# Denominators spread by DMA, a projection bank lent to score units, FFN rows moved, and a shifted pass shared with GpSimd

## The chip, the cores and the metric

The kernel runs on one core of one Trainium2 chip. The metric is the device time of one execution in microseconds (us); lower is better. Times are medians of several executions, and a profile is one execution of its own.

## The reference

`x` is 2048 tokens of 640 values (bf16). The output is `x` plus an attention part plus a feed-forward part (FFN), both on the same normalised `xn`.

```python
def _A_ref(x, wq, wk, wv, wo):
    B, S, D = x.shape
    H = 32
    Dh = D // H
    q = (lambda x, *d: x.transpose(*d))((x @ wq).reshape(B, S, H, Dh), 0, 2, 1, 3)
    k = x @ wk
    v = x @ wv
    scores = jnp.einsum("bhqd,bkd->bhqk", q, k) * (Dh ** -0.5)
    p = _softmax(scores, axis=-1)
    o = jnp.einsum("bhqk,bkd->bhqd", p, v)
    return (lambda x, *d: x.transpose(*d))(o, 0, 2, 1, 3).reshape(B, S, H * Dh) @ wo
...
    h = jnp.einsum("bsd,df->bsf", x, w1) + b1
    r = jnp.where(h > zero, h, zero)
    h = r * r
    out = jnp.einsum("bsf,fd->bsd", h, w2) + b2
...
xn = _layernorm(x, axis=-1)
return x + _A_ref(xn, A_wq, A_wk, A_wv, A_wo) + _B_ref(xn, B_w1, B_b1, B_w2, B_b2)
```

There are 32 query heads of 20 values and a single key and value head; F is 1536. The heart of the work is 32 x 2048 x 2048 exponentials.

## The kernel before

The queries are cut into 4 chunks of 512 tokens (`qc`) and the heads into 8 groups of 4 (`g`); a chunk and a group make one of 32 **blocks**. A block has 16 **tiles**, one for each 128 keys, and a tile has 4 **units**, one for each head: a score matrix of 128 keys by 512 queries, which fills one bank of PSUM. There are 2048 units (L728).

Two engines turn scores into probabilities. *A tiles* go to ScalarE: `S_QK` (L738) makes two or three units in neighbouring banks, and one ACTIVATE (`S_EXP`, L790) takes the exponential of all of them into `PT`. *D tiles* go to VectorE. `S_D` (L820) puts one unit at a time in a bank of its own, `S_P1` (L875) converts it to an integer in `T8`, whose bits read as bf16 are a rough power of two, and `S_PH` (L901) makes four shifted copies of the whole tile of 2048 columns in `PB`. The PV product weighs the four with `PH_W`, so that their errors cancel. `QUOTA` says how many tiles of each block are D tiles, 115 of 512.

PSUM has 8 banks. 0 to 2 and 3 to 5 are two rotating sets for `S_QK`; the third bank of each (`XD` = 2, `DB` = 5) serves either an exponential of three banks or a D unit. `PVB` = 6 gathers the PV products of a block (`S_PV`, L967) and `MB` = 7 serves the **projection rows**, taken by `S_MISC` (L1049) from a list in order of due position: queries (QT, 31 after the first), the FFN's first product (FFN, 48), output rows (OUT, 24) and the last chunk's first halves (P1, 8). Each ends in an evacuation by VectorE.

At the end of a block `norm` (L984) divides the PV sum by its denominator, a row of the same sum: VectorE transposes PSUM to `Tn` (L987) and takes reciprocals (L991), GpSimd multiplies in two pieces (L993), and VectorE transposes back to `OTn` (L1013). GpSimd also squares the FFN's hidden rows, two pieces each (L617). Output rows add the residual from `x_sb`, which stays in SBUF.

The order of all instructions on all engines is worked out as the program is written, by a planner (`Sched`, L99) with fixed durations; each engine then runs its list in order and waits on semaphores. GpSimd's pieces are marked `under`: the planner starts each together with a long VectorE instruction that is not marked `port` (`beneath`, L223). Shifted passes are marked `port` and are not planned beside a GpSimd piece.

Of the kernel before, what the change touches and what calls it, by code (L numbers as in the profile page):

```python
# [6 lines left out]
F32 = mybir.dt.float32  # L7
# [33 lines left out]
QUOTA = [1, 3] + [4, 3, 4] * 9 + [4, 4, 4]  # L41
RING = 20
NT8 = 3
NPB = 5
NQS = 4
EVP = 1
DLEAD = 0.45
DWAIT = 120.0
DALONE = 1500.0
DBEHIND = (1.5, 0.0)  # L50
QLATE = 0.15
PG, PAT = 4, 28.4

SEM_NS = 60.0
PE_WIN = 3420.0
PE_MISC = 9000.0
# [28 lines left out]
class Req:  # L85


    def __init__(self, alts, deps, prio, name="", mode=None, deadline=None, rows=None, after=0.0, cols=0.0, even=False, port=False, under=False):
        self.alts = alts if isinstance(alts, list) else [alts]
        self.deps, self.prio, self.name, self.mode = deps, prio, name, mode  # L90
        self.deadline, self.rows, self.after = deadline, rows, after
        self.cols, self.even, self.port, self.under = cols, even, port, under
# [7 lines left out]
class Sched:  # L100
# [17 lines left out]

    def room(self, t, c):
        tot = self.load(t) + c  # L120
        for s_, c_ in self.win:
            if tot <= PE_MISC:
                break
            if s_ > t - PE_WIN:
                tot -= c_
                t2 = s_ + PE_WIN
                t = max(t, t2)
        return t
# [19 lines left out]
    def run(self):  # L148
        while self.streams:
# [7 lines left out]
            cands = []  # L157
            for st in self.streams:
                r = st[1]
                if isinstance(r, Until):  # L160
                    continue
                rr = r() if callable(r) else r
                if rr is None:
                    continue
                deps = rr.deps() if callable(rr.deps) else rr.deps
                if deps is None or rr.under:
                    continue
                t0 = max([d.done + SEM_NS for d in deps] + [rr.after])
                best = None
                for k, (eng, dur, lat, ins) in enumerate(rr.alts):  # L170
                    est = max(self.free[eng], t0)
                    if eng == "pool" or rr.port:
                        est = max(est, self.port)
                    if rr.even:
                        est = self.room(est, rr.cols)
                    if eng == "pe":
                        dur = self.pe_cost(rr, dur)
                    if best is None or est + dur < best[0]:
                        best = (est + dur, est, dur, k, eng)
                cands.append((best[1], best[2], rr, deps, best[3], best[4], st))  # L180
            if not cands:
                raise RuntimeError("stuck at %.0f: %s" % (self.now, [s[2] for s in self.streams]))
# [70 lines left out]
    def resolve(self, newsem):  # L253
# [37 lines left out]
        for e in self.ENG:  # L291
            n = 0
            for op in self.lists[e]:
                if op.dma is not None:
                    op.sig, op.sem, op.amt, op.val = True, newsem("d_" + op.dma), 16, 16
                elif op.sig:
                    n += 1
                    op.sem, op.amt, op.val = sems[e], 1, n

    def emit(self, eng, e):  # L300
        for op in self.lists[eng]:
# [7 lines left out]
            for f in op.ins:  # L309
                ins = f(e)  # L310
            if op.sig and op.ins:
                ins.then_inc(op.sem, op.amt)
# [5 lines left out]
def bass_parallel_sum__grouped_kv_mqa__dense_activation_squared_relu__prompt_kernel(nc, A_x, A_wq, A_wk, A_wv, A_wo, B_x, B_w1, B_b1, B_w2, B_b2, out):  # L318
    es = ExitStack()
    with es:  # L320
# [3 lines left out]
        x_sb = sb("x_sb", [128, ST, D], BF16)  # L324
# [21 lines left out]
        PB = sb("PB", [128, NPB, HPG, 512], I16)  # L346
        Tn = sb("Tn", [128, 2, 512], F32)
        rd = sb("rd", [128, 2, 16], F32)
        T2 = sb("T2", [128, 2, 512], BF16)
# [37 lines left out]
        def dma(eng, name, fn, deps, land):  # L387
            def gen():
                op = yield Req((eng, 60.0 if eng == "sp" else 500.0, land, [fn]), deps, 0, name)
                op.dma = name  # L390
                done[name] = op
            sc.spawn(gen(), name)
# [131 lines left out]
        def groups(gl, n, b_, deps, p, name, m=32, gdeps=None):  # L524
            v = None
            for k, (L, R) in enumerate(gl):
# [3 lines left out]
                elif gdeps is not None:  # L530
                    dd = dd + gdeps[k]
                v = yield Req(("pe", PE512 if n > 400 else PE320, (PE512 if n > 400 else PE320) + PELAT, col4(L, R, n, b_, k == 0, k == len(gl) - 1, m)),
                              dd, p, name, mode="col", cols=512.0 if n > 400 else 320.0, even=p >= 3)
# [89 lines left out]
        olast = {}  # L623

# [14 lines left out]
        def out_tail(v, st, hh, in1, b_, extra=()):  # L639
# [5 lines left out]
            olast[(st, hh)] = w  # L645
            if (st, 1 - hh) in olast:
# [8 lines left out]
        def u_OUT(qc, st, hh, b_):  # L655
# [7 lines left out]
            yield from out_tail(v, st, hh, x_sb[:, st, cs], b_)  # L663

        def u_P1(st, hh, gs, b_):
# [5 lines left out]
            v = yield Req(("dve", 450.0, 491.0, [lambda e: e.tensor_tensor(out=part[:, st % 4, cs], in0=ps[:, b_, 0:320], in1=x_sb[:, st, cs], op=ALU.add)]), [v], EVP, f"PE1_{st}_{hh}")  # L671
            done[f"PP{st}_{hh}"] = v
            bank[b_].last = [v]
# [7 lines left out]
        def u_FULL(st, hh, b_):  # L681
# [4 lines left out]
            yield from out_tail(v, st, hh, x_sb[:, st, cs], b_)  # L686
# [51 lines left out]
        def S_QK():  # L738
            k = 0
            slot = 0  # L740
            while apos[0] < len(aunits):
# [4 lines left out]
                n = 2 if busy[b3] or ("DBfree" if b3 == DB else "XDfree") not in done or d_behind() > DBEHIND[k % 2] else 3  # L746
# [64 lines left out]
        mbusy = [0]  # L811
        gates = [b + m / float(QUOTA[b]) - DLEAD for b, m, t in dtiles] + [float(NBLK)]

        def d_behind():
            p = pos()
            want = sum(4.0 * min(1.0, max(0.0, (p - gates[n]) / (gates[n + 1] - gates[n]))) for n in range(len(dtiles)))
            return want - nd[0]
        phq = []

        def S_D():  # L820
            todo = list(enumerate(dtiles))
            opened = []
            while todo or opened:
# [10 lines left out]
                def poll():  # L834
                    fb = [x for x in (DB, XD) if not busy[x] and (open3[x] or "QKend" in done) and bank[x].last is not None]
                    if not fb:
# [48 lines left out]

        def S_PH():
            for want in range(len(dtiles)):
# [5 lines left out]
                op = None  # L893
                for j in range(NPH):
                    k = (n * NPH + j) % NPB

                    def deps():
                        if pbres[k].last is None:
                            return None
                        return [acc[-1]] + pbres[k].last  # L900
                    op = yield Req(("dve", 600.0, 640.0, [lambda e, j=j, k=k, s=s: e.tensor_scalar(out=PB[:, k, :, :], in0=T8[:, s, :, :], scalar1=PH_D[j], scalar2=0.5,  # L901
                                                                                             op0=ALU.add, op1=ALU.mult)]), deps, 4, "PH", port=True)
                    pbres[k].last = None
                    pv_items[b].append(("D", t, (j, k), op))
                t8res[s].last = [op]
# [5 lines left out]
        def S_FILL():  # L911
# [4 lines left out]
            while "QKend" not in done:  # L916
                def poll():
# [7 lines left out]
                    if not pv_open[0]:  # L925
                        fb = [x for x in (MB, DB) if not (busy[DB] or not open3[DB] if x == DB else mbusy[0]) and "DBfree" in done and max(o.done for o in bank[x].last) + SEM_NS <= t + 40.0]
# [57 lines left out]
        def norm(b, pv):  # L984
            qc, g = divmod(b, G)
            a = b % 2
            v = yield Req(("dve", 700.0, 717.0, [lambda e: e.transpose(out=Tn[:, a, :], in_=ps[:, PVB, :])]), (lambda: get(*([f"NB{b - 2}"] if b >= 2 else [])) and [pv] + get(f"NB{b - 2}") if b >= 2 else [pv]), 0, f"N1_{b}")  # L987
            bank[PVB].last = [v]
            if b == NBLK - 1:
                done["PVend"] = True  # L990
            w = yield Req(("dve", 160.0, 234.0, [lambda e: e.reciprocal(out=rd[:, a, :], in_=Tn[:, a, DH:512:32])]), [v], 1.5, f"N2_{b}")  # L991
            def n3(e, c0, c1):
                return e.tensor_tensor(out=T2[:, a, 32 * c0:32 * c1].rearrange("p (c d) -> p c d", d=32), in0=Tn[:, a, 32 * c0:32 * c1].rearrange("p (c d) -> p c d", d=32),  # L993
                                       in1=rd[:, a, c0:c1].rearrange("p (c o) -> p c o", o=1).to_broadcast([128, c1 - c0, 32]), op=ALU.mult)
            if b == NBLK - 1:
                w = yield Req(("dve", 650.0, 688.0, [lambda e: n3(e, 0, 16)]), [w], 1.5, f"N3_{b}", port=True)
            else:
                r = w
                w = yield Req(("pool", 540.0, 600.0, [lambda e: n3(e, 0, 8)]), [r], 0, f"N3_{b}", under=True)
                w = yield Req(("pool", 540.0, 600.0, [lambda e: n3(e, 8, 16)]), [r], 0, f"N3_{b}", under=True)  # L1000

            def deps():
                dd = [w]
                if b < 2:
                    dd += done["junk"]
                if qc >= 2:
                    names = [f"O{qc - 2}_{st}_{hh}" for st in range(4 * qc - 8, 4 * qc - 4) for hh in range(2)]
                    o = get(*names)
                    if o is None:
                        return None  # L1010
                    dd += o
                return dd
            w = yield Req(("dve", 690.0, 707.0, [lambda e: e.transpose(out=OTn[:, qc % 2, g, :], in_=T2[:, a, :])]), deps, 1.5, f"N4_{b}")  # L1013
# [16 lines left out]
        for qc in range(QC):  # L1030
            for f in range(FT):
                at = 1.0 + (FT * qc + f) * 0.5
# [4 lines left out]
        for qc in range(QC - 1):  # L1037
            for k in range(8):
                st, hh = 4 * qc + k // 2, k % 2
                need = [f"NB{qc * G + g}" for g in range(G)] + [f"H{qc}_{f}" for f in range(FT)] + ["wo", "w2"]  # L1040
                U(8 * (qc + 1) + 0.35 + k * 0.5, f"OUT{st}_{hh}", need, lambda b_, qc=qc, st=st, hh=hh: u_OUT(qc, st, hh, b_))
        q3 = QC - 1
        for k in range(8):
            st, hh = 4 * q3 + k // 2, k % 2
            need = [f"NB{q3 * G + g}" for g in range(PG)] + [f"H{q3}_{f}" for f in range(FT)] + ["wo", "w2"]
# [3 lines left out]
        def S_MISC(b_, until=None):  # L1049
            while units:  # L1050
# [16 lines left out]
                for j in range(len(units)):  # L1067
                    if units[j][2].startswith("QT") and units[j][0] <= pos() - QLATE and have(*units[j][3]):
                        i = j
                        break  # L1070
                u = units.pop(i)
# [21 lines left out]
        def S_MISC2():  # L1093
            yield from S_MISC(DB, lambda: have("K3", "V3") or not units or units[0][0] > -1)
            done["DBfree"] = True

# [25 lines left out]
        sc.spawn(S_PH(), "PH")  # L1122
        sc.spawn(S_PV(), "PV")
# [55 lines left out]
```

## Time and profile before

| | us |
|---|---|
| median of 3 executions | 755.69 (754.64 to 756.87) |
| the profiled execution, its own time | 755.73 |
| its span, first to last instruction | 753.9 |
| first exponential starts | 16.2 |
| last exponential ends | 743.5 |
| matmuls of the three kinds at L521 with `w_sb` or `wo_pad` | 85.2 + 77.7 + 54.2 |
| two transposes of the normalisation (L987, L1013) | 22.7 + 22.5 |
| GpSimd: squares, products of the normalisation | 58.4 + 37.9 |

"Busy" is the time in which an engine had at least one instruction of the group running. The mean of one instruction is longer than its share of the busy time, since an instruction starts before the one ahead of it has ended. The granted TensorE clock is 0.998 over the span. Transfers are small after the weights are loaded in the first 40 us: some 1 to 11 GB/s.

### The profile page before, as it was taken

The page shows a single profiled execution, that of the slowest core. Times are in us where ns is not written, and L with a number is a line of the kernel's source. Part 1 is how long each engine was busy: PE and PEld are TensorE (multiplying, and loading weights), DVE is VectorE, ACT ScalarE, POOL GpSimd, SP SyncE. Part 2 cuts the span into 40 slices and gives each one's busy share as a digit, 9 for nine tenths or more (in the row PEclk, how much of TensorE's full clock was granted, in tenths as well). Part 3 has the DMA queues.
Part 4 walks back from the last instruction along what each step waited for, and adds up shares of the span by engine and source line. Part 5 has one row for each costly group of instructions (what it writes and reads, how often), then busy time and mean ns, then how long its engine had stood idle before and what let it go on. Part 6 is the DMA issues. An engine that isn't in the chain of part 4 may idle for free.

```text
span 753.9 us, 22837 instructions
## 1 busy us (share of the span) xinstructions
PE 725.3 (96%) x10243; PEld 234.6 (31%) x10243; DVE 702.5 (93%) x1222; ACT 734.0 (97%) x756; POOL 113.1 (15%) x200
## 2 busy tenths in 40 slices
PE   8999999999999999999999999999999999999996
PEld 3422222222233333332223333333223333333333
DVE  6789999999998998999999989989999998899995
ACT  5999999999999999999999999999999999999994
POOL 4321111111011111012221001101222100000000
PEclk9999999999999999999999999999999999999999
DMA  8600000000000000000000000000000000000001
GB/s 257 184 2 1 2 2 2 1 2 2 1 3 10 2 10 2 10 2 10 2 2 3 10 3 10 2 10 10 2 2 2 5 7 11 11 11 2 3 2 37
DMA packets 9412, 12.33 MB, mean 16 GB/s; under 512 B 1761, under 2 KB 8674, under 8 KB 9314
## 3 DMA queue, kind: packets, MB, share of 16 engines
q1 hardware_dynamic: 8002, 10.82, 4.5%
q8 instruction: 80, 1.31, 0.8%
q10 hardware_dynamic: 1312, 0.05, 0.1%
q14 instruction: 18, 0.15, 0.1%
HBM read 8.25 MB, written 2.62 MB: 14 GB/s over the span
## 4 chain that ended last, share of the span: by engine, by line
ACT 84%; PE 15%; DVE 1%; issue 0%; POOL 0%; DVEq 0%; POOLq 0%
ACT PT L790 84%; PE ps L521 4%; PE ps L967 4%; PE ps L728 4%; PE ps L440 1%; DVE out_sb L642 0%; PE ps L915 0%; DVE kT L545 0%; PE ps L510 0%; DVE Tn L987 0%; DVE OTn L1013 0%; DVE T L993 0%; DVE xnT L505 0%; POOL hT_tmp L422 0%; DVEq L320 0%
## 5 line engine op out<-in xcount | busy, mean ns | idle before, releaser
L790 ACT ACTIVATE PT<-ps 128x1024 bf16<-128x1024 f32 (+2 forms) x733 | 725.8, 1182 | 1.6 <-PE ps L728 1.5
L875 DVE TENSOR_SCALAR T<-ps 128x512 uint16<-128x512 f32 x460 | 302.9, 678 | 24.1 <-PE ps L728 23.0
L728 PE MATMUL ps<-qT,kT 20*128 20x512 bf16 x2048 | 287.6, 384 | 19.9 <-ACT PT L790 16.2
L901 DVE TENSOR_SCALAR PB<-T 128x2048 int16<-128x2048 uint16 x460 | 299.8, 685 | 0.9
L967 PE MATMUL ps<-PB,vp 128*32 128x512 bf16 x1840 | 166.7, 382 | 1.1 <-DVE PB L901 0.6
L728 PEld LDWEIGHTS ps<-qT,kT 20*128 20x128 bf16 x2048 | 71.3, 91 | 283.4 <-ACT PT L790 271.7
L967 PE MATMUL ps<-PT,vx 128*32 128x512 bf16 x1588 | 157.7, 389 | 0.0
L617 POOL TENSOR_TENSOR big<-hT_tmp 128x256 bf16<-128x256 bf16 x96 | 58.4, 614 | 306.4 <-DVE PB L901 154.7
L521 PE MATMUL ps<-w_sb,big 128*32 128x320 bf16 x1536 | 85.2, 301 | 0.0
L993 POOL TENSOR_TENSOR T<-Tn,rd 128x256 bf16<-128x256 f32 x62 | 37.9, 617 | 285.5 <-DVE PB L901 212.8
L521 PE MATMUL ps<-xnT,w_sb 128*32 128x512 bf16 x960 | 77.7, 382 | 0.3 <-DVE out_sb L642 0.2
L967 PEld LDWEIGHTS ps<-PT,vx 128*32 128x32 bf16 x1588 | 40.5, 93 | 82.8 <-issue 81.5
L967 PEld LDWEIGHTS ps<-PB,vp 128*32 128x32 bf16 x1840 | 44.8, 95 | 45.3 <-issue 16.3
L521 PE MATMUL ps<-wo_pad,OTn 128*32 128x320 bf16 x1024 | 54.2, 301 | 0.8 <-DVE OTn L1013 0.8
L521 PE MATMUL ps<-xnT,wq_sb 128*20 128x512 bf16 x640 | 51.2, 380 | 0.0
L521 PEld LDWEIGHTS ps<-w_sb,big 128*32 128x32 bf16 x1536 | 36.7, 96 | 28.1 <-issue 15.4
L607 DVE TENSOR_SCALAR hT_tmp<-ps,b1col 128x512 bf16<-128x512 f32 x48 | 35.5, 739 | 4.3 <-PE ps L521 3.8
L521 PEld LDWEIGHTS ps<-wo_pad,OTn 128*32 128x32 bf16 x1024 | 24.6, 96 | 18.5 <-issue 7.4
L521 PEld LDWEIGHTS ps<-xnT,w_sb 128*32 128x32 bf16 x960 | 21.8, 95 | 22.0 <-issue 10.6
L912 PE MATMUL ps<-kT,zeros 128*32 128x512 bf16 x276 | 24.9, 381 | 0.0
L987 DVE STREAM_TRANSPOSE Tn<-ps 128x512 f32<-128x512 f32 x32 | 22.7, 710 | 1.0 <-PE ps L967 0.9
L579 DVE TENSOR_SCALAR qT<-ps 128x512 bf16<-128x512 f32 x31 | 21.2, 685 | 2.5 <-PE ps L521 2.0
(56 smaller groups left out, 169.7 us busy)
## 6 DMA issues: line engine op xcount, KB each, us to landing
w_sb<-in_B_w_dram SPq DMA_DIRECT2D x2, 1920.0 KB, 11.8
out_dram<-out_sb SPq DMA_DIRECT2D x16, 160.0 KB, 1.8
x_sb<-in_A_x_dram SPq DMA_DIRECT2D x3, 640.0 KB, 8.9
wq_sb<-in_A_wq_dram SPq DMA_DIRECT2D x1, 800.0 KB, 6.4
wo_pad<-in_A_wo_dram SPq DMA_DIRECT2D x4, 200.0 KB
x_sb<-in_A_x_dram SPq DMA_DIRECT2D x2, 320.0 KB, 4.0
wk_c<-in_A_wk_dram ACTq DMA_DIRECT2D x1, 25.0 KB, 3.8
wv_c<-in_A_wv_dram ACTq DMA_DIRECT2D x1, 25.0 KB, 4.6
```

Of the source, the lines that this page charges most:

```text
L521: return lambda e: e.matmul(ps[32 * j:32 * j + m, b_, 0:n], Lj, R, start=first, stop=last, tile_position=(0, 32 * j))
L579: alts = [("dve", 620.0, 660.0, [lambda e: e.tensor_scalar(out=dst, in0=ps[:, b_, :], scalar1=QSCALE, scalar2=None, op0=ALU.mult)])]
L607: v = yield Req(("dve", 690.0, 750.0, [lambda e: e.tensor_scalar(out=hT_tmp[:, k, :], in0=ps[:, b_, :], scalar1=b1col[:, f:f + 1], scalar2 ...
L617: w = yield Req(("pool", 540.0, 600.0, [lambda e, hs=hs: e.tensor_tensor(out=h2T[:, qc % 2, f, hs], in0=hT_tmp[:, k, hs], in1=hT_tmp[:, k, ...
L728: ins.append(lambda e, i=i, b=b, t=t, h=h: e.matmul(ps[:, b0 + i, :], kT[32 * h:32 * h + DH, t * 128:(t + 1) * 128], qT[32 * h:32 * h + DH ...
L790: op = yield Req(("act", d_, d_ + 100.0, [lambda e, slot=slot, n=n, b0=b0: e.activation(out=PT[:, slot:slot + n, :], in_=ps[:, b0:b0 + n, ...
L875: op = yield Req(("dve", 600.0, 660.0, [lambda e, s=s, h=h, bk=bk: e.tensor_scalar(out=T8[:, s, h, :], in0=ps[:, bk, :], scalar1=OFFS, sca ...
L901: op = yield Req(("dve", 600.0, 640.0, [lambda e, j=j, k=k, s=s: e.tensor_scalar(out=PB[:, k, :, :], in0=T8[:, s, :, :], scalar1=PH_D[j], ...
L912: fill = [(lambda e, h=h: e.matmul(ps[32 * h:32 * h + 32, PVB, :], zeros32[:, :], kT[:, 0:512], start=False, stop=False, tile_position=(0, ...
L967: ins = [(lambda e, h=h, first=first, last=last: e.matmul(ps[32 * h:32 * h + 32, PVB, :], lhs, rhs[h], start=first, stop=last, tile_positi ...
L987: v = yield Req(("dve", 700.0, 717.0, [lambda e: e.transpose(out=Tn[:, a, :], in_=ps[:, PVB, :])]), (lambda: get(*([f"NB{b - 2}"] if b >= ...
L993: return e.tensor_tensor(out=T2[:, a, 32 * c0:32 * c1].rearrange("p (c d) -> p c d", d=32), in0=Tn[:, a, 32 * c0:32 * c1].rearrange("p (c ...
```

## The change

Four parts and the constants that go with them.

1. **More tiles for VectorE.** `QUOTA` becomes four in 29 of 32 blocks, 122 tiles in all; `T8` gets a fourth buffer and `PB` a sixth. `PB` now lies over `x_sb`, so the residual is read from HBM once more, in 16 transfers.
2. **Denominators by DMA.** The PV sum is copied instead of transposed. Four DMAs spread the row of denominators over partitions, a reciprocal is taken, four DMAs gather it, four more broadcast it to 32 partitions each; then GpSimd multiplies straight into `OTn`. Both transposes go, save for the last block.
3. **Banks.** A D unit may take `MB` when no projection row is due soon. At most two D units may wait for VectorE (`GIVE`); an exponential is held to two banks only where a D unit is due and none is waiting (`OUTM`). FFN rows get new due positions (`FAT`, `FSTEP`). The rule that spaced projection groups on TensorE goes.
4. **Shared pass.** For some tiles, one at a time, GpSimd makes the fourth shifted copy in six pieces of 341 or 342 columns. Work marked `under` is now also planned into gaps of VectorE.

```diff
-QUOTA = [1, 3] + [4, 3, 4] * 9 + [4, 4, 4]
+QUOTA = [1,3]+[4]*29+[2]
-NT8 = 3
-NPB = 5
+NT8 = 4
+NPB = 6
+SHARE = True
+NCUT = 6
+PHP = 560.0
-DLEAD = 0.45
+DLEAD = .2
-DBEHIND = (1.5, 0.0)
+FAT = (0.8, 4.0, 12.2, 20.2)
+FSTEP = 0.2
+MBD = 2
+GIVE = 2
+OUTM = (1,1)
...
+                if rr.under:
+                    eng, dur, lat, ins = rr.alts[0]
+                    est = max(self.free[eng], t0, self.port, self.free["dve"])
+                    below.append((est, dur, rr, deps + ([self.last_port] if self.last_port is not None else []), 0, eng, st))
+                    continue
...
+            idle = min([c[0] for c in cands if c[5] == "dve"] + [1e12])
+            cands += [c for c in below if c[0] + c[1] <= idle + 50.0]
...
-                n = 2 if busy[b3] or (...) not in done or d_behind() > DBEHIND[k % 2] else 3
+                n = 2 if busy[b3] or (...) not in done or wants() and nd[0] - nd[1] < OUTM[k % 2] else 3
...
+        def misc_slack():
+            return MBD > 0 and pos() < MBEND and not any(u[0] <= pos() + MBSLACK and have(*u[3]) for u in units[:6])
...
-                    if not fb:
+                    if not busy[MB] and not mbusy[0] and misc_slack() and nd[0] - nd[1] < MBD:
+                        fb.append(MB)
+                    if not fb or nd[0] - nd[1] >= GIVE:
                         return None
...
+                share = SHARE and not php and dtiles[n][1] < QUOTA[b] - 1 and b < NBLK - 1
...
+        def S_PHP():
+            cuts = [2048 * i // NCUT for i in range(NCUT + 1)]
...
+                for i in range(NCUT):
+                    c0, c1 = cuts[i], cuts[i + 1]
+                    op = yield Req(("pool", PHP, PHP + 60.0, [lambda e, c0=c0, c1=c1, k=k, s=s: e.tensor_scalar(
+                        out=PB[:, k, :, :].rearrange("p h n -> p (h n)")[:, c0:c1], in0=T8[:, s, :, :].rearrange("p h n -> p (h n)")[:, c0:c1],
+                        scalar1=PH_D[j], scalar2=0.5, op0=ALU.add, op1=ALU.mult)]), [acc[-1]] + old, 2, "PHP", under=True)
...
-            v = yield Req(("dve", 700.0, 717.0, [lambda e: e.transpose(out=Tn[:, a, :], in_=ps[:, PVB, :])]), ...)
+            v = yield Req(("dve", 640.0, 700.0, [lambda e: e.tensor_copy(out=Tn[:, a, :], in_=ps[:, PVB, :])]), ...)
+            dma("sp", f"da{b}", [(lambda e, h=h: e.dma_start(dn[32 * h:32 * h + 32, a, :], Tn[32 * h + DH:32 * h + DH + 1, a, :].rearrange("p (r c) -> p r c", c=16))) for h in range(HPG)], [v], 2300.0)
+            w = yield Req(("dve", 90.0, 160.0, [lambda e: e.reciprocal(out=rd[:, a, :], in_=dn[:, a, :])]), [done[f"da{b}"]], 1.5, f"N2_{b}")
+            dma("sp", f"db{b}", [... Rr[32 * h:32 * h + 1, :] ..., rd[32 * h:32 * h + 32, a, :] ... for h in range(HPG)], ..., 2300.0)
+            dma("sp", f"dc{b}", [... Rb[32 * h:32 * h + 32, a, :], Rr[32 * h:32 * h + 1, :] ... for h in range(HPG)], ..., 2600.0)
+            for i in range(2):
+                c = slice(256 * i, 256 * i + 256)
+                w.append((yield Req(("pool", 540.0, 600.0, [lambda e, c=c: e.tensor_tensor(out=OTn[:, qc % 2, g, c], in0=Tn[:, a, c], in1=Rb[:, a, c], op=ALU.mult)]), ..., under=True)))
...
-                at = 1.0 + (FT * qc + f) * 0.5
+                at = FAT[qc] + f * FSTEP
```

## The prediction

> **What bounds the kernel now.** I read the page's busy shares first, then the chain that ended last, then the groups kept apart by shape, then the stages one by one.
>
> ```profile
> PE 725.3 (96%) x10243; PEld 234.6 (31%) x10243; DVE 702.5 (93%) x1222; ACT 734.0 (97%) x756; POOL 113.1 (15%) x200
> ...
> ACT 84%; PE 15%; DVE 1%; issue 0%; POOL 0%; DVEq 0%; POOLq 0%
> ...
> L790 ACT ACTIVATE PT<-ps 128x1024 bf16<-128x1024 f32 (+2 forms) x733 | 725.8, 1182 | 1.6 <-PE ps L728 1.5
> L875 DVE TENSOR_SCALAR T<-ps 128x512 uint16<-128x512 f32 x460 | 302.9, 678 | 24.1 <-PE ps L728 23.0
> L901 DVE TENSOR_SCALAR PB<-T 128x2048 int16<-128x2048 uint16 x460 | 299.8, 685 | 0.9
> ```
>
> Three engines are over 90% busy, so the share alone decides nothing. ScalarE's exponentials do: 725.8 us of work with 1.6 us of idle time ahead of them in a span of 753.9. VectorE, second, idles 24.1 us ahead of L875 alone.
>
> ```profile
> L790 ACT ACTIVATE PT<-ps 128x1024 bf16<-128x1024 f32 x609 | 583.1, 1110 | 1.6 <-PE ps L728 1.5
> L790 ACT ACTIVATE PT<-ps 128x1536 bf16<-128x1536 f32 x123 | 187.6, 1542 | 0.0
> ```
>
> A three-bank exponential lasts 1542 ns and a two-bank one 1110: 432 ns for a bank. 1588 banks by 0.432 are 686.0 us; the other 39.8 us over 733 instructions are 0.054 us for each. Time therefore falls in two ways: fewer banks, or more banks in one instruction.
>
> ```profile
> core 0: us, PE busy (x) PEld busy (x) DVE busy (x) ACT busy (x) POOL busy (x), PEclk, DMA share, GB/s
> 120.00:220.00 100.00, 94.92 (x1203) 26.31 (x1203) 95.74 (x160) 100.00 (x104) 15.29 (x25) 1.00 0.01 2
> ...
> 521.00:570.00 49.00, 48.28 (x617) 13.54 (x617) 48.92 (x83) 49.00 (x52) 13.92 (x23) 1.00 0.01 2
> ```
>
> Even from 521 to 570, where twelve FFN rows crowd in and VectorE is busy 48.92 of 49 us, ScalarE loses nothing.
>
> ```profile
> PEld ps L728 <- ACT PT L790: 271.7, 687, 1.2
> POOL T L993 <- DVE PB L901: 212.8, 42, 21.4
> ```
>
> TensorE stands ready at 687 score groups and waits 271.7 / 687 = 0.395 us for ScalarE to free the bank. That is the slack that lateness on TensorE uses up before ScalarE feels it.
>
> **ScalarE's sum.** The quota list adds up to 115 tiles before and 122 after. Seven tiles, 28 banks, go to VectorE and GpSimd: 1560 banks by 0.432 are 673.9 us. The number of instructions hangs on how often a third bank is free. Before, 460 shifted score units forced 609 two-bank exponentials, 1.32 each. Now some units sit in the projection bank. A QT row in the timeline held it 3.9 us (308.3 to 312.2), an OUT row about 7.3. With 79 QT and FFN rows and 32 OUT and P1 rows that is 308 + 234 = 542 us of the 727 us between first and last exponential, so a quarter is free, and I let a quarter of 488 units go there. The other 366 at 1.32 force 483 two-bank instructions, 966 banks; 594 banks are left for 198 three-bank ones. 681 instructions by 0.054 are 36.8 us. The sum is 710.7 against 725.8: **15.1 us less**. The bounds: all two-bank (780) gives 9.8 us less, all three-bank (520) 23.8.
>
> **VectorE's sum**, which must fit under it. Busy per instruction from the rows: L875 302.9 / 460 = 0.658, L901 299.8 / 460 = 0.652, the two transposes 0.710 and 0.702, the reciprocal 0.238.
> - 28 more conversions +18.4 and 28 more shifted passes +18.3.
> - 31 blocks lose two transposes and a reciprocal, -31 x 1.650 = -51.2, and gain a copy from PSUM (no row; nearest L875 in shape and source, 0.658) and a reciprocal of the same size (0.238): +27.8. Bounds for the copy are the fastest 128x512 row and the slowest, 0.63 to 0.74: 3 us at most.
> - Fourth passes that GpSimd takes. 89 tiles qualify (not the last of a block, not the last block). GpSimd's pieces are set beneath long VectorE instructions that read PSUM: 488 conversions, 31 QT, 48 FFN, 31 copies = 598 places, less 96 squares and 62 normalisations = 440, by six = 73 tiles. One tile at a time and some 14 free places a block make it at most every other tile, so I take 50: -32.6. Bounds 0 and 89.
>
> One piece is 341 columns. No row shows it; the nearest are GpSimd's L566 (80 columns, 475 ns) and L494 (640 columns, 876 ns), which put 341 at about 0.66 us, as long as the conversion above it (0.658). A shifted pass just behind a piece is then held a little: L901's median is 684 ns and its longest 729, so 45 ns at 150 of 300 pieces is 6.8 us. All in all 702.5 - 19.3 + 6.8 = 690.0 us. VectorE's idle time that cannot go: 7 us ahead of 30 us, 8 from 30 to 120, 3 in the last 9, and 1% of the rest. Its floor is **about 716 us**, 23 under ScalarE's 738.8, so ScalarE remains the bound. With no pass shared the floor is 742, and VectorE takes over by 3 us.
>
> [...]
>
> **The denominators' DMAs.** Each block now issues twelve on SP, in three legs of four; each leg waits for the one before, and the plan gives them 2.3, 2.3 and 2.6 us. SP had 16 issues after the first 25 us; 372 more by the 0.33 us of an output issue are 123 us of SP time, hidden. The 16 reloads of x share it. Queued behind a waiting leg on SP are only output stores (four slots, reused tens of us later) and those reloads. What is not hidden: VectorE's reciprocal waits in order for the first leg, with P1, and so score banks, behind it; GpSimd's two products wait for the third, with squares (FFN evacuations wait for them) and shared pieces (TensorE waits) behind them. No row shows a small copy inside SBUF. The nearest landings are the output's 1.8 us and the narrow weight's 3.8. With three earlier issues of 0.33 a leg takes 2.8 to 4.8 us, so it is 0.5 to 2.5 late. I take 0.5, since the long row stood behind the start's megabytes: 31 x 0.5 = 15.5 us, inside VectorE's 23. [...]
>
> **At nothing:** the pacing rule for TensorE that goes (its limit of 9000 columns lies over the 8208 that fit at 2.4 columns a ns in 3420 ns, by the plan's own constants); 21 more PV groups of four at 0.091 us a matmul, 7.6 us, covered by the 0.395 us waits and by 52 fewer score groups, and worth 7.6 if that cover goes; the lent x buffer, free before the first shifted pass at 43.5 us; the moved FFN rows, of which 12 in 49 us already cost ScalarE nothing. The first exponential (16.2 us) and what follows the last (743.5 to 753.9) I leave.
>
> **Sum.** 753.9 - 15.1 = 738.8 for the profiled span; that execution took 755.73 and the median is 755.69, so 1.8 on top: **740.6 us**.
>
> **Rivals.**
> 1. *The reciprocal blocks VectorE* (slower). If the first leg is late by L, VectorE's floor is 716 + 31 L; over 753.9 from L = 1.2 us. Halfway between the bounds, L = 1.5, it gives 716 + 46.5 + 1.8 = 764. For it: twelve dependent small transfers a block, and VectorE full. Against: 1.8 us for a whole output tile. 0.12.
> 2. *Pieces outlast their cover*, so PV groups of the shared passes come late and TensorE, in order, holds up the scores. At L494's 0.876 six pieces end 1.3 us late; less 0.395 of slack that is 0.9 at each of 50 tiles, 45 us at worst, half of it 763. Against: GpSimd's products repeat at 615 to 618 ns. 0.07.
> 3. *The lent bank gives nothing*: projection rows keep it, and 488 units at 1.32 force 644 two-bank instructions, which leave 272 banks for 91 wide ones. 735 by 0.054 are 39.7 us; 673.9 + 39.7 = 713.6, 12.2 less: 743.5. For it: 111 rows and a quarter of the time at most. 0.12.
> 4. *FFN crowding*: rows every 0.2 of a block while four tiles a block are due. Four bursts of 2.4 blocks put some 2.6 us a block more on a full VectorE, 25 us; its buffers of four tiles absorb part, and a third reaches ScalarE: 749. Against: the stage of 521 to 570. 0.08.
> 5. *Gain and loss cancel*: legs late near 1 us leave 755. 0.06.
>
> **How the numbers follow.** The forecast (733 to 746) has 0.55. This measurement cannot tell 0.3%, 2.3 us, from no change. Faster: 0.55 + 0.12 + 0.08 = 0.75; same 0.06; slower 0.19. The range goes from 731 (three-bank exponentials nearly throughout) to 759, which leaves out most of rivals 1 and 2.
>
> **What would show it.** Right: 1560 banks in some 650 to 710 exponentials, under 5 us of idle time ahead of them, VectorE near 690 us, shifted passes down to about 438 and some 300 GpSimd pieces of 0.6 to 0.7 us. Wrong: VectorE idle ahead of the reciprocal by more than 1 us a block for a DMA (rival 1); score or PV weight loads waiting for GpSimd (rival 2); three-bank exponentials under 145 (rival 3); idle time on ScalarE in the FFN bursts (rival 4).

## The result, and the profile after

The changed kernel takes 977.87 us (median of 4, 972.8 to 981.31) against 755.79: 1.2933 times as long, with a 95% interval of 1.2865 to 1.3001. The forecast was 740.6. The profiled execution took 981.31 us, with a span of 979.5. Single executions of some kernels below are over 1.5% longer at a lower granted clock; the times leave these out, which leaves one execution in e2, e3 and e12.

From the page of the changed kernel: busy shares, the granted clock in 40 slices, and the groups that answer to those shown of before (busy us, mean ns | idle us ahead, releaser).

```profile
PE 858.8 (88%) x10255; PEld 245.7 (25%) x10255; DVE 708.3 (72%) x1191; ACT 746.9 (76%) x762; POOL 297.8 (30%) x536
...
PEclk9996977787787878898679888977878798959989
...
L811 ACT ACTIVATE PT<-ps 128x1024 bf16<-128x1024 f32 (+1 forms) x739 | 738.7, 1090 | 215.7 <-PE ps L749 213.8
L903 DVE TENSOR_SCALAR T<-ps 128x512 uint16<-128x512 f32 x488 | 323.5, 683 | 130.1 <-PE ps L749 129.4
...
L1035 PE MATMUL ps<-pbx,vp 128*32 128x512 bf16 x1952 | 216.1, 454 | 97.4 <-POOL pbx L968 88.4
L939 DVE TENSOR_SCALAR pbx<-T 128x2048 int16<-128x2048 uint16 x432 | 293.2, 710 | 3.5 <-PE ps L1035 1.9
L968 POOL TENSOR_SCALAR pbx<-T 128x341 int16<-128x341 uint16 x336 | 166.8, 519 | 256.5 <-DVE pbx L939 254.9
...
L1084 POOL TENSOR_TENSOR OTn<-Tn,Rb 128x256 bf16<-128x256 f32 x62 | 54.3, 898 | 289.6 <-DMA Rb<-Rr 276.7
...
L1074 DVE RECIPROCAL rd<-dn 128x16 f32<-128x16 f32 x31 | 7.8, 252 | 35.2 <-DMA dn<-Tn 35.1
```

The exponentials themselves take 738.7 us where they took 725.8; the new time is idle time, 215.7 us ahead of them against 1.6, nearly the whole loss of 222. Read the releasers backwards. ScalarE waits for scores (L749); TensorE waits at PV groups for GpSimd's shared pieces (L968); GpSimd waits 276.7 us ahead of its products for the broadcast `Rb<-Rr`. No engine is the bound.

One stall, from the timeline (start, us, instructions merged):

```profile
435.88 1.86 POOL L1084 TENSOR_TENSOR OTn<-Tn,Rb 128x256 bf16<-128x256 f32 x2 [11.05 <-DMA Rb<-Rr]
...
437.71 2.24 POOL L968 TENSOR_SCALAR pbx<-T 128x341 int16<-128x341 uint16 x4
...
439.92 2.06 POOL L629 TENSOR_TENSOR big<-hT_tmp 128x256 bf16<-128x256 bf16 x2
441.96 2.70 POOL L968 TENSOR_SCALAR pbx<-T 128x341 int16<-128x341 uint16 x6
442.93 0.62 PE L1035 MATMUL ps<-pbx,vp 128*32 128x512 bf16 x4 [4.42 <-POOL pbx L968]
...
444.13 1.02 ACT L811 ACTIVATE PT<-ps 128x1024 bf16<-128x1024 f32 x1 [4.80 <-PE ps L749]
```

GpSimd stands 11.05 us at the products, then works off its queue in order: products, four pieces, squares, more pieces. TensorE waits 4.42 us for pieces whose tile VectorE had converted long before. The stages around it:

```profile
core 0: us, PE busy (x) PEld busy (x) DVE busy (x) ACT busy (x) POOL busy (x), PEclk, DMA share, GB/s
425.00:439.00 14.00, 13.51 (x178) 3.79 (x170) 13.55 (x24) 13.97 (x15) 3.12 (x5) 1.00 0.47 34
439.00:443.00 4.00, 0.07 (x4) 0.07 (x4) 2.51 (x3) 0.32 (x1) 4.00 (x7) 0.65 0.00 0
443.00:450.00 7.00, 7.00 (x55) 1.33 (x55) 2.48 (x4) 3.97 (x4) 1.65 (x4) 0.50 0.01 1
```

The stall has a second half. While TensorE stands, its granted clock falls, and it is 0.50 for the next 7 us: TensorE is busy throughout and still feeds ScalarE for only 3.97 of 7 us. Of 979 windows of 1 us in this trace, 622 show a clock of 1.00 and 308 one of 0.50. If the other 49 only mix the two, a mean of 0.831 means (1 - 0.831) x 2 x 979.5 = 331 us at half speed. The clock fell 1.7 us into the wait: 0.65 over the four us from 439 means full speed until 440.2, if it fell once, and the wait had begun at 438.5. A wait of 1.65 us elsewhere in this trace was also followed by 13 us at half speed (the wait in the timeline, then the stage behind it):

```profile
300.47 0.60 PE L749 MATMUL ps<-qT,kT 20*128 20x512 bf16 x1 [1.65 <-DVE T L903]
...
301.00:314.00 13.00, 13.00 (x125) 3.42 (x128) 8.91 (x14) 7.59 (x8) 1.59 (x3) 0.50 0.51 34
```

The DMAs' median time from issue to landing:

```profile
Rb<-Rr SPq DMA_DIRECT2D x124, 64.0 KB, 5.7
...
out_dram<-out_sb SPq DMA_DIRECT2D x16, 160.0 KB, 2.1
dn<-Tn SPq DMA_DIRECT2D x124, 2.0 KB, 1.7
Rr<-rd SPq DMA_DIRECT2D x124, 2.0 KB, 1.7
```

The issues of one block on SP:

```profile
447.35 2.40 SPq L1072 DMA_DIRECT2D dn<-Tn  x4
451.20 2.44 SPq L1075 DMA_DIRECT2D Rr<-rd  x4
454.83 3.14 SPq L1078 DMA_DIRECT2D Rb<-Rr  x4
```

A small copy lands in 1.7 us, but SP takes 0.6 us to issue each (four in 2.40 us), so the first two legs take 3.6 us from first issue to last landing, not 2.3 (medians of 31 blocks). The third, the broadcast, takes 9.4, not 2.6. A block's legs are 16.6 us long where the plan has 7.2.

Late work on GpSimd also falls beside VectorE's shifted passes, which the plan keeps apart from it. Durations in ns, shortest, median and longest:

```profile
L939 DVE TENSOR_SCALAR pbx<-T x432: 629/684/1219, 46.2 to 958.4; 128x2048 int16<-128x2048 uint16 x144
...
L1084 POOL TENSOR_TENSOR OTn<-Tn,Rb x62: 718/730/2062, 71.0 to 962.6; 128x256 bf16<-128x256 f32 x62
```

The 78 passes that overlap a GpSimd instruction by over 50 ns last 837 ns on average, the other 354 last 682; the 30 products beside a pass last 1080, the other 32 last 726. Over all passes that is 12 us on VectorE, small beside the loss.

### The profile page after: what moved, and what is told of

Its sections match the earlier page's. It is cut to its first block, busy times and chain, and to the rows that moved or that the text cites. A ratio compares the mean times of both kernels' runs of the same rounds, so it can differ in the third digit from the quotient of the medians.

```text
span 979.5 us, 23561 instructions
## 1 busy us (share of the span) xinstructions
PE 858.8 (88%) x10255; PEld 245.7 (25%) x10255; DVE 708.3 (72%) x1191; ACT 746.9 (76%) x762; POOL 297.8 (30%) x536
## 4 chain that ended last, share of the span: by engine, by line
PE 35%; DMA 26%; POOL 12%; DVE 11%; SPq 11%; issue 3%; ACT 2%; DVEq 0%; POOLq 0%
DMA Rb<-Rr 17%; PE ps L1035 13%; PE ps L749 11%; PE ps L533 10%; POOL pbx L968 6%; DMA Rr<-rd 5%; DMA dn<-Tn 5%; SPq L1078 4%; POOL OTn L1084 4%; SPq L1072 4%; DVE T L903 4%; DVE pbx L939 3%; SPq L1075 3%; POOL big L629 2%; ACT PT L811 2%
## 5 line engine op out<-in xcount | busy, mean ns | idle before, releaser
L811 ACT ACTIVATE PT<-ps 128x1024 bf16<-128x1024 f32 (+1 forms) x739 | 738.7, 1090 | 215.7 <-PE ps L749 213.8
L903 DVE TENSOR_SCALAR T<-ps 128x512 uint16<-128x512 f32 x488 | 323.5, 683 | 130.1 <-PE ps L749 129.4
L749 PE MATMUL ps<-qT,kT 20*128 20x512 bf16 x2048 | 329.9, 435 | 11.3 <-DVE T L903 5.9
L1035 PE MATMUL ps<-pbx,vp 128*32 128x512 bf16 x1952 | 216.1, 454 | 97.4 <-POOL pbx L968 88.4
L939 DVE TENSOR_SCALAR pbx<-T 128x2048 int16<-128x2048 uint16 x432 | 293.2, 710 | 3.5 <-PE ps L1035 1.9
L968 POOL TENSOR_SCALAR pbx<-T 128x341 int16<-128x341 uint16 x336 | 166.8, 519 | 256.5 <-DVE pbx L939 254.9
L749 PEld LDWEIGHTS ps<-qT,kT 20*128 20x128 bf16 x2048 | 74.4, 93 | 337.6 <-ACT PT L811 188.0
L1084 POOL TENSOR_TENSOR OTn<-Tn,Rb 128x256 bf16<-128x256 f32 x62 | 54.3, 898 | 289.6 <-DMA Rb<-Rr 276.7
L533 PE MATMUL ps<-xnT,w_sb 128*32 128x512 bf16 x960 | 98.9, 467 | 0.6 <-DVE qT L591 0.2
L1035 PEld LDWEIGHTS ps<-pbx,vp 128*32 128x32 bf16 x1952 | 51.3, 100 | 167.7 <-POOL pbx L968 95.9
L1070 DVE COPY Tn<-ps 128x512 f32<-128x512 f32 x31 | 21.3, 687 | 31.8 <-PE ps L1035 31.6
L533 PEld LDWEIGHTS ps<-xnT,w_sb 128*32 128x32 bf16 x960 | 23.3, 104 | 32.2 <-issue 23.4
```

The costliest lines, as they stand in the source:

```text
L533: return lambda e: e.matmul(ps[32 * j:32 * j + m, b_, 0:n], Lj, R, start=first, stop=last, tile_position=(0, 32 * j))
L749: ins.append(lambda e, i=i, b=b, t=t, h=h: e.matmul(ps[:, b0 + i, :], kT[32 * h:32 * h + DH, t * 128:(t + 1) * 128], qT[32 * h:32 * h + DH ...
L811: op = yield Req(("act", d_, d_ + 100.0, [lambda e, slot=slot, n=n, b0=b0: e.activation(out=PT[:, slot:slot + n, :], in_=ps[:, b0:b0 + n, ...
L903: op = yield Req(("dve", 600.0, 660.0, [lambda e, s=s, h=h, bk=bk: e.tensor_scalar(out=T8[:, s, h, :], in0=ps[:, bk, :], scalar1=OFFS, sca ...
L939: return Req(("dve", 600.0, 640.0, [lambda e, j=j, k=k, s=s: e.tensor_scalar(out=PB[:, k, :, :], in0=T8[:, s, :, :], scalar1=PH_D[j], scal ...
L968: op = yield Req(("pool", PHP, PHP + 60.0, [lambda e, c0=c0, c1=c1, k=k, s=s: e.tensor_scalar(out=PB[:, k, :, :].rearrange("p h n -> p (h ...
```

## The experiments

All start from the changed kernel unless told otherwise. The last two columns are from the profiled execution; those of e3 and e12 took 908.11 and 800.94 us.

| run | edit | us | against before (95%) | idle ahead of exponentials, us | clock |
|---|---|---|---|---|---|
| (changed) | | 977.87 | 1.2933 (1.2865 to 1.3001) | 215.7 | 0.831 |
| e1_plan | all legs planned as measured | 751.53 | 0.9942 (0.9922 to 0.9963) | 7.7 | 0.997 |
| e2_noshare | no shared passes | 813.79 | one execution | 57.3 | 0.968 |
| e3_ports | rows on four other partitions | 885.8 | one execution | 143.9 | 0.872 |
| e4_oldnorm | no DMAs, old transposes | 754.49 | 0.9984 (0.9974 to 0.9993) | 10.9 | 0.998 |
| e5_one | short legs, planned as measured | 745.68 | 0.9863 (0.9848 to 0.9877) | 2.8 | 1.0 |
| e6_nobank | e1, bank not lent | 751.24 | 0.9934 (0.9918 to 0.9949) | 5.7 | 1.0 |
| e8_third | third leg alone planned long | 814.39 | 1.0772 (1.0679 to 1.0864) | 65.1 | 0.943 |
| e9_oldffn | e1, FFN rows where they were | 759.7 | 1.0057 (1.0033 to 1.0082) | 6.1 | 0.998 |
| e10_thirdlate | first two legs planned right | 927.86 | 1.2289 (1.2242 to 1.2336) | 167.2 | 0.843 |
| e11_late2 | e5, third leg 2.1 us shorter in plan | 754.96 | 0.9995 (0.9984 to 1.0007) | 9.6 | 0.998 |
| e12_late4 | e5, third leg 4.1 us shorter in plan | 784.5 | one execution | 49.0 | 0.946 |
| e13_recip | e8, first leg planned right too | 750.82 | 0.9943 (0.992 to 0.9966) | 4.4 | 0.999 |

**Plan or load?**

```diff
-            dma("sp", f"da{b}", [... for h in range(HPG)], [v], 2300.0)
+            dma("sp", f"da{b}", [... for h in range(HPG)], [v], 3800.0)
...
-                [w] + ([] if b < 1 else [done[f"dc{b - 1}"]]), 2300.0)
+                [w] + ([] if b < 1 else [done[f"dc{b - 1}"]]), 3800.0)
...
-                [done[f"db{b}"]] + old(), 2600.0)
+                [done[f"db{b}"]] + old(), 9600.0)
```

> The changed kernel, but the planner is told what the three DMA legs measured there (3.68, 3.6 and 9.4 us from the first issue to the instruction that waits) instead of 2.3, 2.3 and 2.6; the same work, another order. Theory A (the legs land 10 us later than planned, GpSimd waits in order for the third, its shared pieces come late, TensorE waits in order for them, its clock halves, ScalarE starves): idle time ahead of the exponentials falls from 215.7 us to under 30, granted clock 0.97 or more, 740 to 765 us. Rival B (the added load itself, on the VectorE and GpSimd ports, the DMA engines or the clock, slows the kernel whatever the order): over 900 us, clock under 0.88.

Measured 751.53 us. The legs are as long as in the changed kernel (the third lands 9.4 us after its first issue in both, median), the same bytes move and GpSimd makes 324 pieces for 336; what differs is the order. That takes away 226 us and the clock's fall with it. Theory A holds, rival B falls. From its page and its waits:

```profile
L811 ACT ACTIVATE PT<-ps 128x1024 bf16<-128x1024 f32 (+1 forms) x739 | 717.8, 1121 | 7.7 <-PE ps L749 5.8
...
POOL OTn L1084 <- DMA Rb<-Rr: 48.2, 12, 21.0
```

**Which way does the lateness travel?** `SHARE = False` in one run; the old `norm` in the other.

> The changed kernel without the shared passes: VectorE makes all four. The DMAs and their planned times are as changed. Theory A: the way from late GpSimd to TensorE is mainly the shared pieces (88.4 us of TensorE's wait), so most of the loss goes: 770 to 830 us, what is left being the late reciprocal on VectorE (35 us) and late squares. Rival A2 (the stall goes through the reciprocal, the squares and the output rows as much): 880 to 960. Rival B: no less than 940, or more, since VectorE has 56 passes more.

> The changed kernel with the old normalisation of transposes and no DMAs for the denominators; tiles, banks, FFN positions and shared passes as changed. Theory A: no stall, clock 0.98 or more, 738 to 750 us, the gain of fewer exponentials on ScalarE, with VectorE 23 us nearer to full than forecast. Rival B: over 900.

Without shared passes, 813.79 us: some 164 us of the loss go, though GpSimd waits longer for the broadcast than in the changed kernel (474.7 us for 276.7). What waits behind it is what matters. What is left holds the late reciprocal (32.2 us of waiting) and the passes that VectorE makes again; the two were not separated. With the old transposes there is no stall, but 754.49 us is a bare 0.16% under before, not the 738 to 750 expected: VectorE is at 703.7 of 753.0 us, and only 71 exponentials have three banks:

```profile
L808 ACT ACTIVATE PT<-ps 128x1536 bf16<-128x1536 f32 x71 | 104.2, 1519 | 0.0
```

So the rest of the change, seven tiles fewer on ScalarE included, gives next to nothing with the transposes in place. With the DMAs, rightly planned, VectorE is at 691.0 us and the time 3 us lower; that its relief is the reason fits, but was not tested by itself.

**Why is the broadcast slow?**

```diff
-[(lambda e, h=h: e.dma_start(Rr[32 * h:32 * h + 1, :]..., rd[...])) ...]
+[(lambda e, h=h: e.dma_start(Rr[36 * h:36 * h + 1, :]..., rd[...])) ...]
...
-... Rr[32 * h:32 * h + 1, :].rearrange("p (o n) -> p o n", o=1).to_broadcast([1, 32, 512])
+... Rr[36 * h:36 * h + 1, :].rearrange("p (o n) -> p o n", o=1).to_broadcast([1, 32, 512])
```

> The changed kernel with the four gathered rows of reciprocals on partitions 0, 36, 72 and 108 instead of 0, 32, 64 and 96; nothing else. If the broadcast is slow because the four source rows lie behind few ports of the memory, the third leg falls from 9.4 us to 5 to 7 and the time by a quarter to a half of the loss, 860 to 920 us. If it is slow by the number of pieces, the issue of 0.6 us each or one partition read 32 times, the leg stays over 9 us and the time between 960 and 990.

```profile
Rb<-Rr SPq DMA_DIRECT2D x124, 64.0 KB, 3.9
```

A landing falls from 5.7 to 3.9 us and the leg from 9.4 to 6.4; the time is 885.8 us. Same bytes, pieces and issues, other source partitions. In the changed kernel a block's four broadcasts land ever later after their issue, 4.6, 5.6, 6.3 and 7.5 us (medians), here after 3.8, 3.8, 3.9 and 4.4: so it matters from which partitions the four read. Why these four do better, no run shows.

**Which leg, which waiting engine?** Only the planned landings differ (us): 2.3, 2.3, 12.4 in the first run; 3.8, 3.8, 2.6 in the second; 3.8, 2.3, 11.1 in the third.

> The changed kernel with only the third leg planned longer, 12.4 us, so that GpSimd's products are planned after everything has landed; the first two legs stay at 2.3 us in the plan, so VectorE's reciprocal still comes 1.4 us late each block. If the loss is GpSimd's wait: 750 to 775 us. If the late reciprocal on VectorE (the forecast's rival 1) carries a large part of it: over 800.

> The changed kernel with the first two legs planned as measured (3.8 us each) and only the third left at 2.6 against 9.4. If the two latenesses add, as the runs with a right third leg (814 us) and with all legs right (751.5) suggest, the third alone is worth 978 - 814 = 164 us: 900 to 930 us, with no wait of the reciprocal over 10 us in all. If the first legs are needed for the third to hurt, under 860.

> As the run with only the third leg planned longer (814 us), but the first leg is planned at its measured 3.8 us too, so that VectorE's reciprocal is no longer planned before its operand lands; the second stays at 2.3 and the third at 11.1 covers it. If the 63 us between 814 and 751.5 are the late reciprocal on VectorE, they go: 748 to 760 us, the reciprocal waiting under 12 us in all. If they are the luck of that plan's order or the second leg, it stays over 790.

With the third leg right and the first two 1.3 us late each, 814.39 us, outside the 750 to 775 expected if the loss is GpSimd's wait. Planning the first leg right too takes it to 750.82. From the waits of the two, in that order:

```profile
DVE rd L1074 <- DMA dn<-Tn: 39.7, 31, 2.8
```

```profile
DVE rd L1074 <- DMA dn<-Tn: 6.7, 9, 2.4
```

So 39.7 us of waiting on VectorE, 1.3 us a block, cost some 63 us of time, 2.0 a block (the 814.39 is the middle of two executions 12 us apart). The third leg alone costs 927.86 - 751.53 = 176 us, and TensorE waits for pieces again:

```profile
PE ps L1035 <- POOL pbx L968: 61.8, 22, 6.6
```

Together 239, against 226 measured for both: two stalls that nearly add. Taken the other way round, each on top of the other, the third leg costs 977.87 - 814.39 = 163 us and the first two 977.87 - 927.86 = 50. Each plan also brings an order of its own, whose share is not known.

**What does a late microsecond cost?** The short legs: one DMA each for the first two, partitions 36 apart, and landings planned at 2.3, 2.3 and 6.7 us; then the same kernel with the last figure cut to 4.6 and 2.6.

```diff
-[(lambda e, h=h: e.dma_start(dn[32 * h:32 * h + 32, a, :], Tn[32 * h + DH:32 * h + DH + 1, a, :]...)) for h in range(HPG)]
+lambda e: e.dma_start(dn[:, a, :], Tn[DH:128:32, a, :].rearrange("h (r c) -> h r c", c=16))
...
+lambda e: e.dma_start(Rr[0:109:36, :].rearrange("h (r c) -> h r c", c=16), rd[:, a, :])
```

> The changed kernel with shorter legs: the first two legs are one DMA each instead of four (2.4 us of issue become about 0.6), the gathered rows stand on partitions 0, 36, 72 and 108, and the planner is told 2.3, 2.3 and 6.7 us. Theory A says that only the difference between plan and landing stalls, not the latency itself: legs of about 2.3, 2.3 and 6.4 us as planned, idle time ahead of the exponentials under 10 us, 745 to 752 us. If fewer, wider DMAs take as long as four (legs over 3 us), the reciprocal and GpSimd wait again and it is 760 to 800.

> The kernel with short legs (745.7 us), with the third leg planned at 4.6 us, 1.8 to 2.1 us too early. Theory A with a price in proportion: a block loses its lateness less about 0.5 us, 31 x 1.5 = 47 us: 780 to 800 us, clock 0.96 or more. If GpSimd's idle time covers it, under 755.

> The same with the third leg planned at 2.6 us, 3.8 to 4.1 us too early. In proportion: 31 x 3.5 = 108 us, 840 to 865 us. If stalls long enough to halve TensorE's clock cost more than their length, over 875 us and a clock under 0.9, so that the second 2 us cost clearly more than the first 2.

The short legs take 1.9, 1.9 and 6.3 us at their shortest, 10.1 in all, and the waits for them fall to 2.2 us over the whole run. At 745.68 us this is the fastest kernel of this study, 10 us under the kernel before. Its page:

```profile
PE 728.7 (98%) x10295; PEld 235.9 (32%) x10295; DVE 688.9 (93%) x1192; ACT 724.3 (97%) x762; POOL 266.3 (36%) x524
...
L812 ACT ACTIVATE PT<-ps 128x1024 bf16<-128x1024 f32 (+1 forms) x739 | 716.1, 1133 | 2.8 <-PE ps L750 1.7
...
L1085 POOL TENSOR_TENSOR OTn<-Tn,Rb 128x256 bf16<-128x256 f32 x62 | 44.1, 729 | 65.5 <-DVE pbx L940 64.8
```

The late runs missed the prices in proportion: 754.96 us, at the edge of "under 755", for 780 to 800, and 784.5 for 840 to 865. I had counted lateness from the third leg alone and forgotten that the first two now land 0.8 us early. Over all three legs, 10.1 us against plans of 9.2 and 7.2, the products were by this estimate 0.9 and 2.9 us late: 9.3 us of time (0.3 a block) and 38.8 us (1.3 a block, one execution). In the third-leg run, with its longer legs, they were 16.6 - 10.2 = 6.4 us late and lost 176 us, 5.7 a block. The first microsecond on the products is nearly free, and its 9.3 us need not be lateness at all, for plans without lateness differ by 6 us (751.53 and 745.68). From 2.9 to 6.4 each microsecond costs about (5.7 - 1.3) / 3.5 = 1.3. On the reciprocal 1.3 us already cost 2.0 a block. The clock goes the same way as the time: 0.998, 0.965 (at 784.5 us) and 0.843. How the loss divides between waiting and the halved clock was not separated.

**The bank and the FFN rows**, both in the kernel with measured legs: `MBD = 0`; and `at = 1.0 + (FT * qc + f) * 0.5`.

> The kernel with the measured legs in the plan (751.5 us), but D units never take the projection bank (MBD = 0). If the lent bank frees third banks, as the forecast reckoned, three-bank exponentials fall from 83 to under 40 and the time rises by 3 to 6 us. If it gives nothing, their number and the time stay within 10 and 2 us.

> The kernel with the measured legs in the plan (751.5 us), but FFN rows at the positions of before (every half block). If the moved rows carry part of the gain, since FFN and output rows then crowd again, 755 to 765 us; if they do nothing, 749 to 754.

Not lending the bank leaves 77 three-bank exponentials instead of 83, and 751.24 us for 751.53: it gives nothing. The old FFN positions cost 8 us, but not where I expected it. The exponentials end at 737.4 us, earlier than with the moved rows (741.6). What follows them:

```profile
core 0: us, PE busy (x) PEld busy (x) DVE busy (x) ACT busy (x) POOL busy (x), PEclk, DMA share, GB/s
...
737.00:758.00 21.00, 17.92 (x521) 13.52 (x512) 6.80 (x13) 0.39 (x1) 0.00 (x0) 1.00 0.11 34
```

521 matmuls are left to the end, where the kernel with moved rows has 200 in its last 10 us: six output half rows are made whole there (L661 with `xres` in the timeline), against one. That the last FFN rows come too late for the output's first halves is the likely reason. In the kernel before, the same positions left no such tail (743.5 to 753.9), so the 8 us arise only together with the rest of the change.

## Why the prediction was wrong

- **The step that failed is the one on the denominators' DMAs.** It priced three legs alike, 2.8 to 4.8 us, and took 0.5 us late. The first leg's 3.6 us lies between those bounds. The third measured 9.4, twice the upper bound: the row of an output store to HBM gave no bound for four broadcasts from one partition each. The issue was 0.6 us, not 0.33. So the term of 31 x 0.5 us should have been 1.3 us a block on the first leg and 6.8 on the third.
- **Its second half failed too.** It named GpSimd's products waiting for the third leg with "shared pieces (TensorE waits) behind them", and gave that no price; only the reciprocal got one. The unpriced path carries 163 to 176 of 226 us.
- **The cover was wrong in kind.** Late microseconds were to be paid from VectorE's 23 us of room, and rival 1 had 716 + 31 L. At 1.3 us late that is 758; the run of the reciprocal alone gave 814. VectorE was busy for only 694.1 us there, so room was not what lacked. As I read it, an order fixed beforehand can't move idle time from elsewhere under a wait: each late block is paid on the spot, first by 0.4 us of TensorE's slack, then by ScalarE, then by the clock.
- **Rivals.** Rival 1 named a real mechanism, worth 50 to 63 us. Rival 2 had the right way (late pieces, late PV groups, TensorE in order) with the wrong cause: the pieces last 480 ns undisturbed, not 0.66 us; they start late. Rival 4 falls: with the rows crowded, 2.8 us of idle time stand ahead of the exponentials once the stall is gone.
- **What held, seen once the stall is gone** (745.68 us against 740.6). VectorE 688.9 us, forecast 690.0, in part by luck: the shifted passes took 284.1 us where their terms give 292.3, and the rest 7 us more than forecast. 324 pieces, 54 tiles; forecast 50. 1560 banks as said. The shifted passes last 692 ns on average, against 685 before.
- **Too large:** the lent bank. 82 three-bank exponentials, not 198; rival 3, which had 91, was right that it gives nothing. 739 instructions instead of 681 are 58 x 0.054 = 3.1 us of the 5 between forecast and the mended kernel.
- **"At nothing":** the moved FFN rows are worth 8 us in the changed kernel, at its end, which I left untouched. The 12 FFN rows from 521 to 570 rightly said that a burst costs ScalarE nothing.

## What to carry to other kernels

Where the order of all engines is fixed beforehand, a duration in the plan is a promise to every engine: one DMA that lands late stops the engine that waits, all that is queued behind it, and whoever needs that (here 11.05 us of GpSimd, then 4.42 of TensorE and 4.80 of ScalarE). So price a new wait along its whole chain, not against the waiting engine's spare time, and measure a transfer of the new shape (source partitions, issues) before planning with it. Latency alone cost little here: legs of 16.6 us, told to the planner, came out 3 us ahead of the old normalisation.

## What was not expected of the hardware

- Four broadcasts of 64 KB inside SBUF land in 5.7 us each (median) from partitions 0, 32, 64 and 96, and in 3.9 from 0, 36, 72 and 108.
- SP needs 0.6 us to issue a small copy inside SBUF, so that one DMA over all partitions instead of four cuts a leg from 3.6 us (median) to 1.9 (shortest).
- GpSimd's product of two full f32 operands of 256 columns takes 729 ns on average with the short legs, against 617 with a repeated one in the kernel before. The mean of 898 in the changed kernel comes from the 30 of 62 that ran beside a shifted pass (1080 ns, longest 2062).
- TensorE's granted clock fell to 0.50 after a wait of 1.65 us (at 298.8) and stayed there for 13 us of uninterrupted work; in the wait from 438.5 it fell after 1.7 us.
- Products about 0.9, 2.9 and 6.4 us late cost 0.3, 1.3 and 5.7 us a block; a reciprocal 1.3 us late costs 2.0.
